# A recurrence with two MLPs behind it: the weights' working word in PSUM, scores masked on half the partitions, decay products stored with time outermost

## The chip, the cores and the metric

The kernel runs on one core of one Trainium2 chip. The core has five engines that run side by side, each through its own list of instructions in order: PE (TensorE, the matmuls), DVE (VectorE), ACT (ScalarE), POOL (GpSimd) and SP (SyncE, which mostly issues DMAs). The metric is the device time of one execution in microseconds (us), as a median of runs.

## The reference

The input `r, k, v, w, a, b` has 4 batches, 8 heads, 768 time steps and 40 channels. A 40 by 40 state per batch and head is carried over time:

```python
y[:, :, t] = einsum('bhd,bhde->bhe', rt, state)
Sa = einsum('bhde,bhe->bhd', state, at)
state = state * wt[:, :, None, :] - einsum('bhd,bhe->bhde', Sa, bt) + einsum('bhd,bhe->bhde', vt, kt)
```

Its output, 3072 tokens by 320, goes through two MLPs. The first is `g(x @ w_in) @ w_out` with 2048 hidden columns and `g(h) = h` for h >= 1, 0 for h <= -1 and (h+1)^2/4 between. The second is `(silu(x @ w_gate) * (x @ w_val)) @ w_out` with 1536. The MLP weights are 64-bit floats in DRAM; everything else is 32 bits.

## The kernel before

Time is cut into 12 chunks (`c`) of 64 steps, and each chunk into 4 super-units (`n`, one for each batch, with 8 heads), 48 in all. A planner (`Plan`) holds all work as tasks with an engine, an estimated cost, what they read and write, and which buffers they use. It simulates the engines from estimates and due times, and so settles the order of instructions on every engine; the kernel is then written out in that order. The due times come from the constants in line 1262. Buffers are handed out from pools; a pool can grow (`K.grow`) once given tasks are over.

The kinds of work:

- `decay_tasks` (lines 661 to 760), for three groups of 4 chunks: running products of the decays `w` and of their reciprocals, on 128 partitions (4 chunks x 32 batch-heads), 32 steps at a time, 40 channels a step. The tiles lie in `wg` and `wv`, the memory of the second MLP's weights, which are therefore loaded later. `last` (lines 713 to 721) copies the products at the chunk ends aside, `store` (723 to 728) writes the products to two DRAM tensors, `was` and `wks`, one pair for each group.
- `p_tasks` (785 to 880), for each n: loads r, k, a, b and, for each pair of n, 64 steps x 16 batch-heads x 40 of `was` and of `wks` (`ldw`, line 805); multiplies, splits into two 16-bit halves, turns, and forms the scores of one n with 8 matmuls (line 850) in a `pg` tile of PSUM, 128 partitions x 512. Line 853 multiplies them by the causal `mask` (which also holds a factor of 2^-6), line 857 copies the lower half to `gf`, from which line 861 stores them to DRAM (`lsd`).
- `inv_tasks` (882 to 942), for each chunk: reads `lsd` back and inverts triangular blocks with 62 small dependent steps on DVE (lines 912 and 917). Only entries right of the diagonal are read. The result goes to DRAM (`tsd`).
- `m_tasks` (970 to 1162), for each n, after the inverse of its chunk: a chain PE, ACT, DVE, PE ... through one `px` tile of PSUM (matmuls of lines 1035, 1045, 1051; ACT 1059, 1070; DVE in `xlo`, `slo`), then the output y and the next state. It reads `was` once for each pair of n (line 996). The first four n use the two `ph` tiles in place of `px`.
- The MLPs: `in1` and `in2` (matmuls of line 1167), the pointwise part on ACT, DVE and POOL (1187 to 1217), `outp` (1231).
- `wpiece` (578 to 641), 58 of them: one piece of weights is loaded as raw 64-bit words (`wr`), turned into 32-bit floats by three DVE bit operations (lines 609, 613, 617) in a 32-bit buffer `wu` in SBUF, then split into 16-bit halves by ACT (636, 629) and POOL or DVE. 28 pieces are 128 partitions x 320, 30 are 512 columns on 128 or 64 partitions. 30 pieces of the second MLP (`late`) wait until all decays are done.

PSUM has eight tiles of 128 x 512 here: two each of `px`, `pg`, `ph` and `po`. DVE and POOL tasks that the planner takes to hold the port that both share are marked `lk`.

Of the kernel before, what the change touches and what calls it, by code (L numbers as in the profile page):

```python
# [8 lines left out]
F32 = mybir.dt.float32  # L9
# [313 lines left out]
def tile_recurrence__then__gated_mlps(  # L323
# [59 lines left out]
    def pst(name, n):  # L383
        ts = [pp.tile([128, 512], F32, name=f"{name}{i}") for i in range(n)]
        K.pool(name, ts)
        return ts
# [60 lines left out]
        K.spare(nm, [mx[:, 5120 + 1024 * i:6144 + 1024 * i].rearrange(  # L447
            "p (h x) -> p h x", h=H)], early)
    K.spare("gf", [mx[:, 7168:8192].bitcast(F32).rearrange("p (h t) -> p h t", h=H)], early)
    pst("px", 2)  # L450
    pst("pg", 2)
    ph = pst("ph", 2)
    po = [pp.tile([128, 512], F32, name=f"po{i}") for i in range(2)]
# [124 lines left out]
    def wpiece(names, key, src, n, m, dst_hi, dst_lo, scale, p, fit, r=()):  # L578

        key = ("w",) + key  # L580
        K.pools["wr"]["fit"][key] = [x for f in fit for x in {
            "low": (0,), "high": (1,), "free": (2,), "late": (3, 4)}[f]]
        K.pools["wu"]["fit"][key] = [x for f in fit for x in {
            "low": (0, 4), "high": (1, 5), "free": (2,), "late": (3,)}[f] if m <= 320 or x < 4]
        raw, ux = [("wr", key)], [("wu", key)]
        shape = list(dst_hi.shape)

        def st():
            return G("wr", key)[0:n, 0:2 * m].bitcast(I32)

        def x(i):
            return st().rearrange("p (b x) -> p b x", x=2)[:, :, i]

        def u():
            return G("wu", key)[0:n, 0:m]

        def u3():
            return u() if len(shape) == 2 else u().rearrange("p (a f) -> p a f", a=shape[1])

        def load(e):  # L600
            o = st()
            if len(shape) == 3:
                o = o.rearrange("p (a f) -> p a f", a=shape[1])
            e.dma_start(out=o, in_=src)

        def bits(q):
            t = u().bitcast(I32)
            if q == 0:
                v_.tensor_scalar(
                    out=t, in0=x(1), scalar1=3, scalar2=0x3FFFFFFF,  # L610
                    op0=ALU.logical_shift_left, op1=ALU.bitwise_and)
            elif q == 1:
                v_.scalar_tensor_tensor(
                    out=t, in0=x(1), scalar=-(1 << 30), in1=t, op0=ALU.bitwise_and,
                    op1=ALU.bitwise_or)
            else:
                v_.scalar_tensor_tensor(
                    out=t, in0=x(0), scalar=29, in1=t, op0=ALU.logical_shift_right,
                    op1=ALU.bitwise_or)

        pool = n == 128 and WSP
        e_, eng, cost = side(pool, m)
        if pool:
            k, scale, scale0 = 4, 1.0, scale
        else:
            k = 3

        def hi():
            s_.activation(out=dst_hi, in_=u3(), func=AF.Copy, scale=scale)

        DMA(load, r=r, w=[(key, 0)], use=raw, p=p, dma=0.00365 * m * n / 128)
        for q in range(3):
            T("DVE", 0.06 + m * (1.04e-3 if q else 0.52e-3), lambda q=q: bits(q), r=[(key, q)], lk=True,
              w=[(key, q + 1)], use=raw + ux, p=p)
        if pool:
            T("ACT", c_s(m), lambda: s_.activation(
                out=u(), in_=u(), func=AF.Copy, scale=scale0), r=[(key, 3)], w=[(key, 4)], use=ux, p=p)
        T("ACT", c_s(m), hi, r=[(key, k)], w=[(key, 5)], use=ux, p=p)
        T(eng, cost, lk=True, emit=lambda: split(dst_lo, u3(), scale, dst_hi, e_), r=[(key, 5)],
          w=[key] + names, use=ux, p=p)  # L640
        return key
# [18 lines left out]

    def decay_tasks(g, p, dp):
        dec[g] = tuple(
            dr.tile([4, BH, C, D], F32, name=f"{nm}{g}") for nm in ("was", "wks"))
        wc = w.rearrange("b h (g c t) e -> g c (b h) t e", g=NG, c=4)[g]
        EC = 16
        e_, eng, cost = side(g, 2 * D)
        for u in range(HC // EC):
# [44 lines left out]

            def last(half=half):
                a = half(0)
                v_.tensor_copy(out=p64[:, g], in_=a[:, 2 * EC + 1])
                for i in range(4):
                    n = 4 * g + i
                    if n:
                        gg, ii = divmod(n - 1, 4)
                        v_.tensor_copy(  # L720
                            out=q0s[32 * ii:32 * ii + 32, gg], in_=a[32 * i:32 * i + 32, 0])

            def store(e, i, l0, l1, half=half, lo=lo, hi=hi):
                dst, h, o, t0 = (
                    (1, 0, 1, lo), (0, 0, EC + 1, hi), (0, 1, 0, lo), (1, 1, EC + 2, hi))[i]
                e.dma_start(
                    out=dec[g][dst].rearrange("q b t e -> (q b) t e")[l0:l1, t0:t0 + EC],
                    in_=half(h)[l0:l1, o:o + EC])

            db = [("db", key)]  # L730
# [6 lines left out]
            if EC * u + EC < HC:  # L737
                T("DVE", 0.15, keep, r=[(key, EC)], w=[("cry", g, u)], use=db, p=pu)
            else:
                T("DVE", 0.5, last, r=[(key, EC)], w=[("dl", g)], use=db, p=pu)  # L740
            T("DVE", 0.33, rec, lk=True, r=[(key, EC)], w=[(key, "r", 0)], use=db, p=pu)
            for k in range(EC - 1):
                T(eng, cost, lambda k=k, back=back: back(k), lk=True, r=[(key, "r", k)],
# [41 lines left out]
    def p_tasks(n, p):  # L785
# [19 lines left out]
        def ldw(i, src, done):  # L805
            DMA(lambda e: e.dma_start(
                out=G("ldp", pp)[0:C, i].rearrange("p j h e -> p (j h) e"),
                in_=src[c % 4, 8 * j:8 * j + 16].rearrange("h t e -> t h e")),
                r=[("dec", c)], w=[done], use=L, p=p - 4, dma=1.06)

        hs = slice(8 * j, 8 * j + 8)
# [35 lines left out]
        def mm():  # L847
# [3 lines left out]

        T("PE", 0.24, mm, r=[(key, "kbT"), ("art", n)], w=[(key, "g")], use=PG + KT + A_, p=p)
        T("DVE", c_v(512, True), lambda: v_.tensor_tensor(
            out=hc(G("pg", key)), in0=hc(G("pg", key)),
            in1=mask.unsqueeze(1).to_broadcast([128, H, C]), op=ALU.mult),
          r=[(key, "g")], w=[(key, "gm")], use=PG, p=p)
        T("ACT", c_s(512), lambda: s_.copy(out=G("gf", key)[C:128], in_=hc(G("pg", key))[C:128]),  # L857
          r=[(key, "gm")], w=[(key, "gf")], use=PG + GF, p=p)

        def st(e, hf):  # L860
            e.dma_start(
# [108 lines left out]
    def m_tasks(n, p):  # L970
# [23 lines left out]
        if j % 2 == 0:  # L994
            ps = slice(8 * j, 8 * j + 16)
            DMA(lambda e: e.dma_start(
                out=G("wa", mp).rearrange("p j h d -> p (j h) d"),
                in_=was[c % 4, ps].rearrange("h t e -> t h e")),
                r=[("dec", c)], w=[(mp, "wa")], use=WA, p=p + 4, dma=1.06)
            if not last:  # L1000
                DMA(lambda e: e.dma_start(
                    out=G("ff", mp)[q].rearrange("p j h d -> p (j h) d"),
# [256 lines left out]
                    out=out[r0:r0 + C, :], in_=o()[64 * q:64 * q + 64]),  # L1259
                    r=[(ok, tt, 1)], w=[("out", c)], use=[("u", uk)], p=p, dma=0.31)  # L1260

    PER, LEAD, PLEAD, DLEAD, WLEAD, ILEAD, WSTEP, LPRI, LSTEP, BP, BI, BM, DP, BD, P1, M1 = 69.67, 10.07, 94.28, 203.97, -27.79, 128.76, 0.3, 0.99, 2.22, -0.71, 2.76, 0.02, 10.0, 113.83, 0.0, 5.0
    SUP = PER / B

    def m0(n):
# [15 lines left out]
    for i in range(NP1):  # L1281
# [4 lines left out]
        for x in ps:  # L1286
            n = len(first)
            first.append(wpiece(
                *x, p=-WLEAD + WSTEP * n, fit=("low", "high", "free") if n < NW1 else ("low", "high")))
    late, low, high = [], list(first), list(first)  # L1290
    free = [("dec", c) for c in range(NCH)] + [("f", c) for c in range(NCH - 1)] + first[:NW1]
    for i, k in W2:
        if k < 2:
# [83 lines left out]
```

## Time and profile before

| | us |
|---|---|
| median of 3 runs | 1157.7 (1156.53 to 1158.95) |
| the profiled execution, its own time | 1156.32 |
| span of the profiled execution, first to last instruction | 1154.6 |

Busy share of the span: PE 79%, ACT 75%, DVE 67%, POOL 51%. The page cuts the span into 40 slices of 28.9 us and gives the busy share of each engine in tenths (9 is 90% or more), then the clock granted to TensorE in tenths of full speed, then the share of the DMA engines that is busy. A name as `L617` is line 617 of the kernel; `xs<-px,xs` says that a tile `xs` is written from `px` and `xs`. PE's records are modelled and a few can be missing, so its busy time is a guide. The waits name the operation that came last before the engine went on.

### The profile page before, as it was taken

The page shows a single profiled execution, that of the slowest core. Times are in us where ns is not written, and L with a number is a line of the kernel's source. Part 1 is how long each engine was busy: PE and PEld are TensorE (multiplying, and loading weights), DVE is VectorE, ACT ScalarE, POOL GpSimd, SP SyncE. Part 2 cuts the span into 40 slices and gives each one's busy share as a digit, 9 for nine tenths or more (in the row PEclk, how much of TensorE's full clock was granted, in tenths as well). Part 3 has the DMA queues.
Part 4 walks back from the last instruction along what each step waited for, and adds up shares of the span by engine and source line. Part 5 has one row for each costly group of instructions (what it writes and reads, how often), then busy time and mean ns, then how long its engine had stood idle before and what let it go on. Part 6 is the DMA issues. An engine that isn't in the chain of part 4 may idle for free.

```text
span 1154.6 us, 29904 instructions
## 1 busy us (share of the span) xinstructions
PE 916.4 (79%) x11328; PEld 748.1 (65%) x11328; DVE 776.4 (67%) x1830; ACT 864.8 (75%) x1628; POOL 587.2 (51%) x756
## 2 busy tenths in 40 slices
PE   0222548426687989999999999999999999999998
PEld 0212436324575778777777777787777877788886
DVE  7888888898889485683775756947758558342211
ACT  1675987867995888987978979889798896763422
POOL 5787875435566546544554545655535432332321
PEclk9999999557799999999999999999999999999999
DMA  9967889869886888688677768875777643311000
GB/s 228 212 175 144 196 148 204 153 143 202 172 163 130 132 130 138 121 137 123 115 121 139 128 104 137 131 140 121 125 129 128 118 89 58 65 34 32 5 15 24
DMA packets 560949, 144.64 MB, mean 125 GB/s; under 512 B 537140, under 2 KB 544820, under 8 KB 560804
## 3 DMA queue, kind: packets, MB, share of 16 engines
q1 hardware_dynamic: 519984, 134.11, 63.1%
q10 hardware_dynamic: 40820, 8.62, 4.8%
q8 instruction: 88, 1.44, 0.5%
q14 instruction: 57, 0.47, 0.1%
HBM read 74.87 MB, written 18.14 MB: 81 GB/s over the span
## 4 chain that ended last, share of the span: by engine, by line
PE 31%; ACT 16%; DVE 12%; issue 5%; DMA 5%; POOL 2%; SPq 1%; ACTq 1%; POOLq 0%; DVEq 0%
PE ph L1167 17%; PE po L1231 11%; DVE pg L917 2%; DVE ub L912 2%; ACT mx L1199 2%; ACT mx L1187 2%; ACT xs L1059 1%; PE pg L1124 1%; ACT vss L1070 1%; ACT mx L1200 1%; DVE xs L539 1%; DVE mx L1217 1%; ACT gf L857 1%; ACT ss L1137 1%; POOL mx L537 1%
## 5 line engine op out<-in xcount | busy, mean ns | idle before, releaser
L537 POOL TENSOR_TENSOR mx<-mx 128x512 f16<-128x512 f32 x168 | 196.3, 1170 | 245.7 <-ACT mx L1187 224.7
L1231 PE MATMUL po<-wo,mx 128*128 128x320 f16 x2016 | 311.8, 301 | 2.3 <-POOL mx L537 1.6
L1231 PEld LDWEIGHTS <-mx 128*128 128x128 f16 x2016 | 189.7, 98 | 70.7 <-POOL mx L537 4.3
L1167 PE MATMUL ph<-mx,w 128*128 128x256 f16 x1536 | 196.0, 281 | 14.8 <-DMA mx<-x 9.3
L1167 PEld LDWEIGHTS <-w 128*128 128x128 f16 x1536 | 149.7, 100 | 40.8 <-issue 14.0
L1167 PE MATMUL ph<-x2t,wv 128*128 128x256 f16 x1152 | 142.4, 274 | 3.4 <-DVE mx L1203 2.6
L1167 PE MATMUL ph<-x2t,wg 128*128 128x256 f16 x1152 | 141.8, 275 | 2.1 <-ACT mx L1213 2.1
L1187 ACT CAST mx<-mx 128x512 f16<-128x512 f32 x168 | 102.8, 615 | 46.0 <-DVE mx L1217 31.6
L1203 DVE SCALAR_TENSOR_TENSOR mx<-ph,mx 128x512 f32<-128x512 f32 x96 | 66.0, 689 | 86.6 <-ACT mx L1200 85.8
L1167 PEld LDWEIGHTS <-wv 128*128 128x128 f16 x1152 | 110.8, 98 | 18.6 <-issue 4.5
L1167 PEld LDWEIGHTS <-wg 128*128 128x128 f16 x1152 | 110.5, 98 | 18.4 <-issue 2.5
L917 DVE TENSOR_TENSOR pg<-pg,ub 128x126 f32<-128x126 f32 (+22 forms) x372 | 96.3, 259 | 9.9
L912 DVE SCALAR_TENSOR_TENSOR ub<-ub,pg 128x126 f32<-128x126 f32 (+22 forms) x372 | 92.4, 248 | 11.3 <-DMA ub<-lsd 1.1
L1217 DVE SCALAR_TENSOR_TENSOR mx<-ph,mx 128x512 f32<-128x512 f32 x72 | 49.5, 687 | 69.4 <-PE ph L1167 64.8
L543 POOL TENSOR_TENSOR ldp<-ldp 128x320 f32<-128x320 f32 (+1 forms) x90 | 78.9, 887 | 29.4 <-ACT ldp L819 17.6
L1059 ACT ACTIVATE xs<-px 32x320 f16<-32x320 f32 x176 | 75.0, 426 | 15.7 <-PE px L1051 6.8
L1070 ACT ACTIVATE vss<-px 32x640 f16<-32x640 f32 x88 | 61.1, 695 | 12.2 <-PE px L1045 10.3
L539 DVE SCALAR_TENSOR_TENSOR xs<-px,xs 32x320 f16<-32x320 f32 x88 | 42.5, 483 | 41.1 <-ACT xs L1059 38.3
L1199 ACT ACTIVATE mx<-ph 128x512 f32<-128x512 f32 x96 | 57.1, 595 | 15.4 <-PE ph L1167 13.9
L539 DVE SCALAR_TENSOR_TENSOR vss<-px,vss 32x320 f16<-32x320 f32 x88 | 43.4, 493 | 31.6 <-ACT vss L1070 25.7
L1200 ACT ACTIVATE mx<-mx 128x512 f32<-128x512 f32 x96 | 60.5, 630 | 3.0
L1213 ACT ACTIVATE mx<-ph 128x512 f32<-128x512 f32 x72 | 42.7, 594 | 24.8 <-PE ph L1167 23.2
(234 smaller groups left out, 1715.9 us busy)
## 6 DMA issues: line engine op xcount, KB each, us to landing
ldv<-in_v_dram SPq DMA_DIRECT2D x86, 80.0 KB
ub<-lsd SPq DMA_DIRECT2D x23, 256.0 KB
wo<-in_moe_w_out_dram SPq DMA_DIRECT2D x16, 320.0 KB
ldp<-in_b_dram SPq DMA_DIRECT2D x23, 160.0 KB
ldp<-wks SPq DMA_DIRECT2D x23, 160.0 KB
out_dram<-mx SPq DMA_DIRECT2D x45, 80.0 KB
wo<-in_moe_w_in_dram SPq DMA_DIRECT2D x7, 512.0 KB
ldp<-in_r_dram SPq DMA_DIRECT2D x22, 160.0 KB
```

What stands on the lines that cost most here:

```text
L537: e.tensor_tensor(out=out, in0=x, in1=hi, op=ALU.subtract)
L539: e.scalar_tensor_tensor(out=out, in0=x, scalar=scale, in1=hi, op0=ALU.mult, op1=ALU.subtract)
L543: e.tensor_tensor(out=out, in0=x, in1=y, op=ALU.mult)
L912: v_.scalar_tensor_tensor(out=t, in0=L()[:, j, j + 1:].unsqueeze(1).to_broadcast([128, nm, ni]), scalar=-(2.0**-10), in1=m[:, 0:nm, j:j + ...
L917: v_.tensor_tensor(out=m[:, 0:nm, j + 1:], in0=m[:, 0:nm, j + 1:], in1=t, op=ALU.add)
L1059: s_.activation(out=xs[32 * i:32 * i + 32], in_=px[32 * hf:32 * hf + 32], func=AF.Copy, scale=-(2.0**-10))
L1070: s_.activation(out=hi2(G("vss", key)[z]), in_=two(hd(G("px", key))[z]), func=AF.Copy, scale=2.0**-8)
L1167: t_.matmul(out=ps, lhsT=wts[:, wi, fs], rhs=xT[:, xi, :], start=(i == 0), stop=(i == len(plan) - 1))
L1187: T("ACT", c_s(512), lambda: s_.copy(out=G("g", key)[:, 0], in_=u2(key)), r=[(key, "u")], w=[(key, "gh")], use=U + GG, p=p)
L1199: s_.activation(out=u2(key), in_=ps2(key), func=AF.Relu, scale=2.0**-8, bias=1.0)
L1200: s_.activation(out=u2(key), in_=u2(key), func=AF.Square, scale=2.0**3)
L1231: t_.matmul(out=ps, lhsT=g[:, x, f, 128 * tt:128 * tt + 128], rhs=wo[:, 2 * i + f, y, :], start=(i == 0 and f == 0 and m == 0), stop=(i == ...
```

## The change

1. One of the two `px` tiles becomes a pool of its own, `pw`, and goes back to `px` once all late weight pieces are done. The first two bit operations of each piece write their word there, and the third reads it from there and writes `wu`. They are no longer marked `lk`, the first one's estimated cost is doubled, and `wu` is taken only at the third.
2. `was` is stored as time x batch-head x channel instead of batch-head x time x channel; `wks` keeps its order. The two loads of `was` then read rows of 16 x 40 numbers, 2560 bytes, instead of 40 numbers, 160 bytes; the stores of `was` write 160 bytes at a time instead of 16 x 160.
3. The copies in `last` go from DVE to ACT.
4. The mask is multiplied onto partitions 0 to 63 alone. ACT copies the lower half straight from the unmasked scores, with the factor 2^-6, and no longer waits for the mask.
5. The constants of the due times: decays 14.66 us earlier (group 0 another 43.73), their two halves 6.14 us apart instead of 10, the late weights due 15.32 us earlier, the first weights 0.46 us apart instead of 0.3, `p_tasks` of chunk 0 due 9.29 us later and of chunk 1 14 us earlier, `m_tasks` of chunk 0 due 9.93 us later. The whole order is planned anew from these.

```diff
-    pst("px", 2)
+    px = pst("px", 2)
+    K.pools["px"]["free"] = px[0:1]
+    K.any("pw", px[1:2], (0,))
...
         def bits(q):
-            t = u().bitcast(I32)
+            t = G("pw", key)[0:n, 0:m].bitcast(I32)
...
             else:
                 v_.scalar_tensor_tensor(
-                    out=t, in0=x(0), scalar=29, in1=t, op0=ALU.logical_shift_right,
+                    out=u().bitcast(I32), in0=x(0), scalar=29, in1=t, op0=ALU.logical_shift_right,
...
-            T("DVE", 0.06 + m * (1.04e-3 if q else 0.52e-3), lambda q=q: bits(q), r=[(key, q)], lk=True,
-              w=[(key, q + 1)], use=raw + ux, p=p)
+            T("DVE", 0.06 + m * 1.04e-3, lambda q=q: bits(q), r=[(key, q)],
+              w=[(key, q + 1)], use=raw + [("pw", key)] + (ux if q == 2 else []), p=p)
...
         dec[g] = tuple(
-            dr.tile([4, BH, C, D], F32, name=f"{nm}{g}") for nm in ("was", "wks"))
+            dr.tile(x + [D], F32, name=f"{nm}{g}")
+            for nm, x in (("was", [C, 4 * BH]), ("wks", [4 * BH, C])))
...
-                v_.tensor_copy(out=p64[:, g], in_=a[:, 2 * EC + 1])
+                s_.copy(out=p64[:, g], in_=a[:, 2 * EC + 1])
...
-                        v_.tensor_copy(
+                        s_.copy(
...
-                    out=dec[g][dst].rearrange("q b t e -> (q b) t e")[l0:l1, t0:t0 + EC],
+                    out=(x if dst else x.rearrange("t b e -> b t e"))[l0:l1, t0:t0 + EC],
...
-            out=hc(G("pg", key)), in0=hc(G("pg", key)),
-            in1=mask.unsqueeze(1).to_broadcast([128, H, C]), op=ALU.mult),
+            out=hc(G("pg", key))[0:C], in0=hc(G("pg", key))[0:C],
+            in1=mask[0:C].unsqueeze(1).to_broadcast([C, H, C]), op=ALU.mult),
...
-        T("ACT", c_s(512), lambda: s_.copy(out=G("gf", key)[C:128], in_=hc(G("pg", key))[C:128]),
-          r=[(key, "gm")], w=[(key, "gf")], use=PG + GF, p=p)
+        T("ACT", c_s(512), lambda: s_.activation(
+            out=G("gf", key)[C:128], in_=hc(G("pg", key))[C:128], func=AF.Copy, scale=2.0**-6),
+          r=[(key, "g")], w=[(key, "gf")], use=PG + GF, p=p)
...
-                in_=was[c % 4, ps].rearrange("h t e -> t h e")),
-                r=[("dec", c)], w=[(mp, "wa")], use=WA, p=p + 4, dma=1.06)
+                in_=was[:, BH * (c % 4) + 8 * j:BH * (c % 4) + 8 * j + 16]),
+                r=[("dec", c)], w=[(mp, "wa")], use=WA, p=p + 4, dma=0.6)
...
-    PER, LEAD, PLEAD, DLEAD, WLEAD, ILEAD, WSTEP, LPRI, LSTEP, BP, BI, BM, DP, BD, P1, M1 = 69.67, 10.07, 94.28, 203.97, -27.79, 128.76, 0.3, 0.99, 2.22, -0.71, 2.76, 0.02, 10.0, 113.83, 0.0, 5.0
+    PER, LEAD, PLEAD, DLEAD, WLEAD, ILEAD, WSTEP, LPRI, LSTEP, BP, BI, BM, DP, BD, P1, M1 = 69.67, 10.07, 94.28, 218.63, -27.79, 128.76, 0.46, -14.33, 2.22, -10.0, 2.76, -9.91, 6.14, 157.56, 14.0, 5.0
...
+    K.grow("px", px[1:2], late)
```

## Rows read from the trace of the kernel before

**Rows 1.** The page's 40 slices: busy tenths of PE and DVE, DMA share.

```profile
PE   0222548426687989999999999999999999999998
DVE  7888888898889485683775756947758558342211
DMA  9967889869886888688677768875777643311000
```

**Rows 2.** Stretches: length, busy PE, weight loads, DVE, ACT, POOL; clock, DMA, GB/s.

```profile
0.00:376.00 376.00, 180.34 (x2268) 143.96 (x2269) 325.02 (x754) 270.03 (x496) 237.55 (x353) 0.88 0.87 174
207.00:269.00 62.00, 17.09 (x371) 15.12 (x370) 57.85 (x141) 43.95 (x88) 20.52 (x24) 0.52 0.82 161
269.00:322.00 53.00, 40.66 (x488) 30.89 (x488) 46.08 (x72) 47.30 (x89) 32.42 (x30) 0.82 0.91 175
376.00:1011.50 635.50, 597.05 (x7709) 489.47 (x7709) 419.27 (x1026) 538.66 (x1028) 311.88 (x365) 0.99 0.71 120
```

**Rows 3.** PE in order of time: first `in1` of chunk 1, first `in2`.

```profile
269.01 8.20 PE L1167 MATMUL ph<-mx,w 128*128 128x256 f16 x48 [4.60 <-DMA mx<-x]
322.00 1.37 PE L1167 MATMUL ph<-x2t,wg 128*128 128x256 f16 x8
```

**Rows 4.** DVE time of lines 609, 613, 617 (in this order), 0 to 376 us.

```profile
0.00:376.00 376.00, 33.40 (x58) 0.88 0.87 174
...
0.00:376.00 376.00, 43.85 (x58) 0.88 0.87 174
...
0.00:376.00 376.00, 45.02 (x58) 0.88 0.87 174
```

**Rows 5.** The chain of waits in order of time, one link: start, length.

```profile
309.12 1.20 DVE wo L617
```

**Rows 6.** DVE in order of time, weight operations without a stall.

```profile
161.24 0.32 DVE L609 TENSOR_SCALAR wo<-wo 128x320 int32<-128x320 int32 x1
...
163.33 0.48 DVE L617 SCALAR_TENSOR_TENSOR wo<-wo 128x320 int32<-128x320 int32 x1
...
166.36 0.42 DVE L609 TENSOR_SCALAR wo<-wo 128x512 int32<-128x512 int32 x1
```

**Rows 7.** Operations with a PSUM operand, to 376 us: ns min/median/max, first and last start.

```profile
L853 DVE TENSOR_TENSOR pg<-pg,mask x18: 679/698/700, 53.6 to 366.3; 128x512 f32<-128x512 f32 x18
...
L873 DVE TENSOR_TENSOR lkt<-pg,lkt x16: 683/684/685, 56.8 to 368.2; 64x512 f16<-64x512 f32 x16
...
L539 DVE SCALAR_TENSOR_TENSOR xs<-px,xs x17: 482/483/485, 165.6 to 335.0; 32x320 f16<-32x320 f32 x17
```

**Rows 8.** A POOL operation in the same stretch, the same columns.

```profile
L543 POOL TENSOR_TENSOR wg<-wg x62: 343/353/800, 34.7 to 143.5; 128x80 f32<-128x80 f32 x62
```

**Rows 9.** The copies of `last` (two lines of DVE), and a small ACT operation.

```profile
L720 DVE COPY wg<-wv x11: 172/179/3108, 27.8 to 145.4; 32x40 f32<-32x40 f32 x11
...
L954 ACT ACTIVATE x<-pf x48: 235/238/245, 135.2 to 1049.3; 64x64 f16<-64x64 f32 x48
```

**Rows 10.** One `px` tile's use, chunk 1: PE and DVE in order of time.

```profile
203.10 0.43 PE L1045 MATMUL px<-xs,tt 96*32 96x40 f16 x8 [0.53 <-DVE xs L539]
...
210.38 0.46 PE L1035 MATMUL px<-vh,lkt 128*128 128x40 f16 x8
...
216.25 0.43 PE L1045 MATMUL px<-xs,tt 96*32 96x40 f16 x8
...
205.00 0.49 DVE L539 SCALAR_TENSOR_TENSOR vss<-px,vss 32x320 f16<-32x320 f32 x1 [0.22 <-ACT vss L1070]
```

**Rows 11.** DMA: the page's main queue; issue times on SP's queue; a landing on the chain.

```profile
q1 hardware_dynamic: 519984, 134.11, 63.1%
...
L726 SPq DMA_DIRECT2D was<-wv x8: 350/430/636, 21.9 to 190.4; - x8
...
L806 SPq DMA_DIRECT2D ldp<-was x21: 587/672/2687, 37.5 to 883.7; - x21
...
987.65 3.21 DMA tsd<-ub
```

More of the change, by code (lines that the diff above doesn't have):

```diff
@@ L584, in wpiece @@
             "low": (0, 4), "high": (1, 5), "free": (2,), "late": (3,)}[f] if m <= 320 or x < 4]
+        K.pools["pw"]["fit"][key] = (0,)
         raw, ux = [("wr", key)], [("wu", key)]
@@ L725, in store @@
                     (1, 0, 1, lo), (0, 0, EC + 1, hi), (0, 1, 0, lo), (1, 1, EC + 2, hi))[i]
+                x = dec[g][dst]
                 e.dma_start(
-                    out=dec[g][dst].rearrange("q b t e -> (q b) t e")[l0:l1, t0:t0 + EC],
+                    out=(x if dst else x.rearrange("t b e -> b t e"))[l0:l1, t0:t0 + EC],
                     in_=half(h)[l0:l1, o:o + EC])
@@ L739, in decay_tasks @@
             else:
-                T("DVE", 0.5, last, r=[(key, EC)], w=[("dl", g)], use=db, p=pu)
+                T("ACT", 0.6, last, r=[(key, EC)], w=[("dl", g)], use=db, p=pu)
             T("DVE", 0.33, rec, lk=True, r=[(key, EC)], w=[(key, "r", 0)], use=db, p=pu)
@@ L807, in ldw @@
                 out=G("ldp", pp)[0:C, i].rearrange("p j h e -> p (j h) e"),
-                in_=src[c % 4, 8 * j:8 * j + 16].rearrange("h t e -> t h e")),
+                in_=src[:, BH * (c % 4) + 8 * j:BH * (c % 4) + 8 * j + 16] if i == 3 else
+                src[BH * (c % 4) + 8 * j:BH * (c % 4) + 8 * j + 16].rearrange("h t e -> t h e")),
                 r=[("dec", c)], w=[done], use=L, p=p - 4, dma=1.06)
```

## The prediction

> **What bounds the kernel now.** I read the page's slices first [rows 1]. From about slice 13 on PE is at 8 or 9 tenths; before it PE is mostly idle while DVE stands at 7 to 9 and the DMA engines likewise. The cut by stretches says the same in microseconds [rows 2]: in 376 us PE is busy for 180, DVE for 325 (86%), ACT for 270, POOL for 238. From 376 to 1011 PE is busy 597 of 635.5 us, and the last five slices are nearly PE alone [rows 1]. So the kernel is two programs: a head of 376 us in which PE waits for weights, decays and the recurrence, and a tail in which PE's own work sets the pace. What the head gives back moves the end nearly one for one, because the tail behind it is the same matmuls and the recurrence is over some 100 us before the end.
>
> Within the head the worst place is 207 to 269 us: PE does 17 us of work at a granted clock of 0.52 (mostly the 1.2 GHz level) after a stretch of sparse matmuls, while DVE is busy 57.85 of 62 us, 93% [rows 2]. PE then waits for the tokens of chunk 1 (269 us) and for the second MLP's weights: `in2` of chunk 0 starts at 322 [rows 3]. All three bit operations of all 58 weight pieces fall into the head; they take 33.40 + 43.85 + 45.02 = 122.3 us, 38% of DVE's time there [rows 4]. The chain of waits, as far as it can be followed back (to 303 us), runs through them too, by a link of 1.20 us for one [rows 5].
>
> **The bit operations.** Undisturbed, an operation on 320 columns takes 0.32 (line 609) or 0.48 us, on 512 columns 0.42 us for line 609 [rows 6]; by the sums the three lines take 0.58, 0.76 and 0.78 on average [rows 4]. Operations on DVE with one operand in PSUM do not vary at all: 512 columns 683 to 685 ns or 679 to 700, 320 columns 482 to 485, over the same 376 us [rows 7]. POOL's decay steps, with everything in SBUF, show the counterpart: median 353 ns and up to 800 [rows 8]. I read this as DVE and POOL holding each other up where DVE's operands all lie in SBUF, and not where one lies in PSUM. After the change each of the three has an operand or its result in PSUM. So 28 pieces x 3 x 0.483 = 40.6 and 30 x 3 x 0.684 to 0.698 = 61.6 to 62.8 make 102 to 103 us; rounded up to 104, that saves 18 of 122. Line 609 itself gets dearer: 28 x (0.48 - 0.32) + 30 x (0.68 - 0.42) = 12 us, already in the 104. Bounds: 20 gained; or 12 lost, if the stalls stay and only line 609's price comes. I take 18, since the rows of the same shape with a PSUM operand are flat.
>
> **The copies of `last`.** DVE loses line 720's 11 copies at 0.18, one of them stalled to 3.1, some 5 us, and three more of about 0.2 from line 715: 5.5 us [rows 9]. ACT gains 14 at about 0.24 [rows 9], 3.4 us, beside other work, as ACT is 72% busy in the head [rows 2]. The new wait: ACT now stands at the end of each decay chain, which POOL runs for groups 1 and 2 at 353 ns a step [rows 8]; behind it on ACT are the copies out of PSUM. Bounds 0 to 3 us for each of the two groups; I take 0, because DVE had no idle time worth naming ahead of these copies.
>
> **Mask and `gf`.** Halving the partitions saves nothing: 64 partitions x 512 take 684 ns, 128 take 698 [rows 7]. `gf` starts one mask earlier, 0.7 us once per chunk on the way to the inverse; of the first four chunks, which PE awaits, 0 to 2.8 us in all. I take 1.
>
> **`was` in DRAM.** The main queue moves 519984 packets and 134.11 MB in 63.1% of 16 engines' span [rows 11], that is 22.4 ns a packet or 13.9 ns for 160 bytes. A load of `was` is 1024 rows of 160 bytes: 0.9 (by bytes) to 1.4 us (by packets) of all 16 engines; after, 64 rows of 2560: 0.1 to 0.9. A store of 128 partitions goes the other way: 128 rows today, 0.2 to 1.8 us, 2048 rows after, 1.8 to 2.9. There are 48 loads but only about 18 in the head, and the equal of 12 such stores, all in the head. So the head gains 0 to 23 us of DMA time and loses 0 to 32; I take nothing there, as the middles nearly cancel. On SP's queue a load's issue falls from 0.67 us towards the 0.43 of a 128-row store, 4 us in the head; 16 stores grow from 0.43 to somewhere between that and twice a load's 0.67, 0 to 15 us over the first 190. For chunk 0 the cover is the gap between its stores, the last of them from `wv` from 21.9 us on, and the first load at 37.5 [rows 11]. If that cover were gone, a store's landing would count whole: 64 KB in runs of 64 bytes landed in 3.21 us [rows 11], so 2048 runs in at most 6.4.
>
> The Trainium skill speaks against this part: "DMA: Bandwidth & Descriptors", section Specifications, says that below 512 bytes the DMA engine reads and rewrites what it writes. The row nearest to it, 1024 writes of 64 bytes in 3.21 us, shows no such price so far; if the rule holds at full weight it is the fourth rival below.
>
> **One `px` tile.** This is the cost. In chunk 1 the first two n hold both tiles and wait for the inverse; the second's first matmul of line 1045 runs at 203.10, while the first n is done at 205.49 [rows 10]. With one tile the second n can only start its chain then, and a chain takes 5.9 us from its first matmul to that point (210.38 to 216.25) [rows 10]. That is 205.5 + 3 to 5.9 = 208.5 to 211.4 instead of 203.1: 5 to 8 us late, and the two n behind it likewise. The next chunk in the head has the same pattern. The delay doesn't add up from chunk to chunk, since each waits for its own inverse. Bounds 0 to 8 us on the start of `in1`; I take 4, as at 93% DVE fills such gaps with work that it owes anyway. No wait is added between pieces: reuse of the PSUM word is in order on DVE.
>
> **The order.** The constants ask for decays, and the second MLP's weights behind them, some 15 us earlier. By how much DVE can comply is bounded by its load. It is 0 in the sum, and a rival.
>
> **Sum.** DVE loses 18 + 5.5 = 23.5 of its 325 us in the head. I pass on 86% of it, its busy share: 20 us, and 1 for `gf`. Less 4 for `px`: 17. The tail I take as it was; shorter loads and an earlier `gf` could touch its 38 us of PE gaps, but nothing there waits for them for long. The profiled execution took 1156.32 us (1154.6 span and 1.7 around it), so 1139; the median lies 1.4 higher: 1140.5.
>
> **Rivals.** (a) *More than that.* If the weights of the second MLP come early enough, `in2` of chunk 0 fills the hole from 215 to 322 us, where PE idles 45 + 12 us. One chunk of it is 96 + 96 matmuls at about 0.27 and some 72 at 0.3, about 73 us, so the hole could be filled; but DVE still owes most of its time. I give 17 + 25 = 42 us, the 25 being less than half of those 57: 1116. For: the low clock there, which would go too. Against: DVE at 93%.
> (b) *DVE was busy but not late.* The chain goes over ACT, PE and landings as well, ACT is busy 72%, and freed DVE time becomes idle time: 2 to 6 us, 1153.
> (c) *The one `px` tile decides, and it is slower.* In a head with the recurrence as the late thing, 8 us are lost for each of two chunks that then do follow each other, and DVE's 23.5 us go unused except for some 8: 16 - 8 = +8, 1165. It decides as soon as `in1` of chunk 1 starts later than 269 us.
> (d) *The small stores are dear.* By bytes from 64 KB in 3.21 us [rows 11], 320 KB would need 16 us. The DMA engines stand at 6 to 9 tenths or more in the first seven slices [rows 1]; if each of the 12 stores took twice 2.9 us of all engines there instead of at most 1.8, 48 us of DMA time would be added, a third of it late, and the gain is eaten: 1157.
> (e) *It doesn't do what it says.* The stalls come from another side than the operands, line 609 gets dearer by 12 us, and 12 - 5.5 = 6.5 us more DVE work, and 4 to 8 for `px`, make 1165.
>
> **How the numbers follow.** Forecast, 1128 to 1151: 0.50. (a) 1105 to 1128: 0.15. (b) 0.14, of which 0.04 is too small to see. (d) 0.04. (c) 0.12 and (e) 0.05. A measurement of this kernel can tell about 0.2%, 2.3 us, from no change. Faster by more: 0.50 + 0.15 + 0.10 = 0.75; same 0.04 + 0.04 = 0.08; slower 0.17. The range leaves out the best part of (a) and the worst of (c) and (e): 1112 to 1163.
>
> **What would show it.** Lines 609, 613 and 617 flat near 0.49 and 0.69 us and 104 us in sum; POOL's maxima smaller; `in1` of chunk 1 before 269 and `in2` of chunk 0 before 322; the last weight piece some 17 us earlier than 376. PE waiting on line 1035 for `slo` of the n before would speak for (c); ACT or landings in place of DVE in the head's waits for (b); late first loads of `was` for (d). The prediction is wrong if DVE's time falls and the second MLP starts no earlier, or if the tail's gaps change: I have taken the tail as fixed, and the new order touches it too.

## The result, and the profile after

The kernel after takes 1166.53 us (median of 4 runs, 1165.09 to 1167.19), the kernel before, run beside it, 1157.86 (1156.53 to 1158.95). The ratio is 1.0068, 95% interval 1.0047 to 1.0089: slower by 0.7%, 8 to 9 us, where 1140.5 was predicted with a range up to 1163.

The part of the forecast on DVE itself came true. The three bit operations by shape, of the kernel after (count | busy us, mean ns of one | idle before); 320 and 512 columns now have one price each, in every line:

```profile
L612 DVE TENSOR_SCALAR px<-wo 128x320 int32<-128x320 int32 x17 | 8.3, 486 | 3.9 <-DMA wo<-in_moe_w_out_dram 3.8
L616 DVE SCALAR_TENSOR_TENSOR px<-wo,px 128x320 int32<-128x320 int32 x17 | 8.4, 491 | 0.3
L612 DVE TENSOR_SCALAR px<-wo 128x512 int32<-128x512 int32 x14 | 9.6, 686 | 3.5 <-DMA wo<-in_moe_w_in_dram 3.4
L620 DVE SCALAR_TENSOR_TENSOR wo<-wo,px 128x512 int32<-128x512 int32 x13 | 8.9, 684 | 0.5
```

The same three lines (612, 616, 620 in this order, once 609, 613, 617) summed from 0 to 376 us, which answers to [rows 4]:

```profile
0.00:376.00 376.00, 34.17 (x58) 0.76 0.90 174
0.00:376.00 376.00, 34.37 (x58) 0.76 0.90 174
0.00:376.00 376.00, 34.00 (x58) 0.76 0.90 174
```

That is 102.5 us, where 104 was predicted and 122.3 stood before. The stretches of the kernel after (length, busy PE, weight loads, DVE, ACT, POOL; clock, DMA share, GB/s), to be read against [rows 2]:

```profile
0.00:376.00 376.00, 172.95 (x2280) 140.30 (x2281) 297.58 (x737) 273.25 (x509) 224.44 (x362) 0.76 0.90 174
207.00:269.00 62.00, 20.07 (x365) 16.58 (x364) 55.17 (x135) 43.13 (x84) 21.64 (x25) 0.54 0.79 144
269.00:322.00 53.00, 37.38 (x466) 28.98 (x464) 45.02 (x77) 47.38 (x90) 28.88 (x33) 0.89 0.84 171
```

DVE is busy for 297.6 us instead of 325.0, 27 less (the prediction: 23.5). POOL, for which the prediction had no term, gains as well: 224.4 instead of 237.6. The last weight operation starts at 352.4 instead of 374.4 us. Yet PE got through 2280 matmuls by 376 us, against 2268: the head is hardly further. The landmarks of [rows 3] in the kernel after, `in1` of chunks 1 and 6 and `in2` of chunk 0 (start, length, idle before it):

```profile
267.19 1.23 PE L1174 MATMUL ph<-mx,w 128*128 128x256 f16 x5 [5.03 <-DMA mx<-x]
...
317.59 1.04 PE L1174 MATMUL ph<-x2t,wg 128*128 128x256 f16 x8
...
693.76 2.53 PE L1174 MATMUL ph<-mx,w 128*128 128x256 f16 x11 [2.82 <-DMA mx<-x]
```

`in1` of chunk 1 comes 1.8 us earlier, `in2` of chunk 0 4.4 us. So 27 us of DVE and 13 of POOL gave 2 to 4. And then the tail loses: `in1` of chunk 6 starts at 693.8 us where it started at 689.1, chunk 7 at 772.4 instead of 762.4, and from there on all is 9 to 11 us late. The tail by stretches, first before, then after (columns as above):

```profile
376.00:690.00 314.00, 291.35 (x3766) 237.53 (x3765) 207.30 (x510) 268.11 (x510) 162.29 (x194) 0.99 0.76 126
690.00:850.00 160.00, 152.36 (x1988) 125.79 (x1987) 107.86 (x261) 139.86 (x268) 84.63 (x99) 1.00 0.77 133
```

```profile
376.00:690.00 314.00, 288.30 (x3707) 234.77 (x3707) 208.05 (x509) 266.57 (x505) 158.61 (x185) 0.99 0.77 124
690.00:850.00 160.00, 147.11 (x1908) 119.93 (x1907) 104.83 (x257) 135.04 (x258) 78.77 (x92) 0.99 0.71 127
```

Behind 376 us the kernel after does 59 and 80 fewer matmuls in these two stretches. What PE lacked is on the page, in the group of the first MLP's matmuls (busy, mean | idle before it and its releaser), before and after:

```profile
L1167 PE MATMUL ph<-mx,w 128*128 128x256 f16 x1536 | 196.0, 281 | 14.8 <-DMA mx<-x 9.3
```

```profile
L1174 PE MATMUL ph<-mx,w 128*128 128x256 f16 x1536 | 191.2, 277 | 29.6 <-DMA mx<-x 18.2
```

`mx<-x` are the turned tokens, the output of the recurrence. PE waits twice as long for them. And the inverses, on which the recurrence waits, are late too; the end of the inverse of each chunk (the last of its 62 steps in the trace, us) and the time of the same execution, with five of the kernels below:

| chunk | 3 | 4 | 5 | 6 | 7 | 11 | time |
|---|---|---|---|---|---|---|---|
| before | 371.7 | 442.0 | 514.9 | 594.4 | 671.9 | 983.5 | 1156.3 |
| after | 370.7 | 448.7 | 532.8 | 610.9 | 682.7 | 995.0 | 1167.1 |
| prio_before | 372.1 | 443.6 | 517.7 | 593.0 | 670.7 | 984.1 | 1157.2 |
| head_before | 372.2 | 440.3 | 517.4 | 593.2 | 670.6 | 988.9 | 1161.2 |
| early_inv | 368.7 | 438.9 | 517.8 | 596.7 | 671.4 | 990.6 | 1161.8 |
| short_third_op | 368.3 | 439.1 | 512.0 | 589.2 | 666.5 | 977.9 | 1151.0 |
| long_second_op | 394.6 | 466.2 | 539.0 | 616.2 | 693.7 | 1005.7 | 1178.4 |

Up to chunk 3 the two kernels are level. The 7 to 18 us at chunks 4 to 6 show behind the head, where no weight piece runs any more, and prio_before, with the same edits, doesn't have them: this is the new order, not the edits. In all seven the execution ends 171 to 173 us behind its last inverse (chunk 11), and so it does in the nine other kernels of this document. Whatever a kernel loses or gains here it has lost or gained by its last inverse; what PE does behind it takes the same time in each, within 2 us. What holds the inverses up is not in these numbers, as their steps stand in DVE's queue between other work.

### The profile page after: what moved, and what is told of

It is laid out like the page before. It is cut to its first block, busy times and chain, and to the rows that moved or that the text cites. A ratio compares the mean times of both kernels' runs of the same rounds, so it can differ in the third digit from the quotient of the medians.

```text
span 1165.4 us, 29896 instructions
## 1 busy us (share of the span) xinstructions
PE 912.2 (78%) x11328; PEld 746.0 (64%) x11328; DVE 751.7 (65%) x1816; ACT 870.4 (75%) x1642; POOL 570.2 (49%) x756
## 5 line engine op out<-in xcount | busy, mean ns | idle before, releaser
L1174 PE MATMUL ph<-mx,w 128*128 128x256 f16 x1536 | 191.2, 277 | 29.6 <-DMA mx<-x 18.2
L1194 ACT CAST mx<-mx 128x512 f16<-128x512 f32 x168 | 102.5, 615 | 51.4 <-DVE mx L1224 28.6
L545 POOL TENSOR_TENSOR ldp<-ldp 64x320 f32<-64x320 f32 (+1 forms) x90 | 76.3, 861 | 15.1 <-ACT ldp L825 9.5
L539 POOL TENSOR_TENSOR x<-pf,x 64x320 f16<-64x320 f32 x48 | 37.9, 789 | 68.2 <-ACT x L960 53.1
L539 POOL TENSOR_TENSOR vss<-ldv,vh 128x320 f16<-128x320 f32 x48 | 38.5, 802 | 59.4 <-ACT vh L1022 36.5
## 6 DMA issues: line engine op xcount, KB each, us to landing
wo<-in_moe_w_in_dram SPq DMA_DIRECT2D x7, 512.0 KB
```

Of the source, the lines that this page charges most:

```text
L539: e.tensor_tensor(out=out, in0=x, in1=hi, op=ALU.subtract)
L545: e.tensor_tensor(out=out, in0=x, in1=y, op=ALU.mult)
L1174: t_.matmul(out=ps, lhsT=wts[:, wi, fs], rhs=xT[:, xi, :], start=(i == 0), stop=(i == len(plan) - 1))
L1194: T("ACT", c_s(512), lambda: s_.copy(out=G("g", key)[:, 0], in_=u2(key)), r=[(key, "u")], w=[(key, "gh")], use=U + GG, p=p)
```

## Experiments: the edits and the order apart

Ratios are to the kernel before, run beside each, with 95% intervals. First the edits without the word in PSUM, in exactly the old order:

```diff
 # the kernel before; was, half mask, gf and last as in the change, the planner's inputs as they were
-                v_.tensor_copy(out=p64[:, g], in_=a[:, 2 * EC + 1])
+                s_.copy(out=p64[:, g], in_=a[:, 2 * EC + 1])
...
-            dr.tile([4, BH, C, D], F32, name=f"{nm}{g}") for nm in ("was", "wks"))
+            dr.tile(x + [D], F32, name=f"{nm}{g}")
```

> The kernel before with parts 2, 3 and 4 of the change in the instructions alone: was with time outermost, the copies of last on ACT, half mask and gf straight from the scores. The planner is told nothing of it (old costs, old dependences), so the order of all tasks is that of the kernel before. Word in SBUF, two px tiles. Theory A: these parts are small by themselves, 1152 to 1159 us. Theory B, if it is the stores, ACT or gf: 1163 or more.

1154.78 us, 0.9989 (0.9972 to 1.0005). The stores of 160 bytes, the longer rows of the loads, `last` on ACT and the half mask together move nothing that can be measured.

Then all edits, but with the priorities that won for the kernel before in place of those that follow from the new constants:

```diff
 # the kernel after, Plan.run
-        prio, best = [t["p"] for t in self.tasks], None
-        for _ in range(self.rounds):
+        prio, best = [x / 1000 for x in PRIO], None   # the old kernel's winning priorities
+        for _ in range(1):
```

> All edits of the change stay (word in PSUM, one px tile in the head, was with time outermost, last on ACT, half mask). Only the priorities by which the planner orders the tasks are those with which it won in the kernel before, task by task, written into the kernel as a list. Theory A (the new order of the recurrence's tasks is what lengthens the tail; the edits themselves are worth something): faster than before, 1140 to 1152 us, with the inverse of chunk 5 ending before 515 us (before: 514.9, after: 532.8). Theory B (the edits cost it: one px tile, or dearer stores, or more on ACT): as slow as the changed kernel, 1162 to 1170.

1156.97 us, 1.0014 (0.9997 to 1.0032), between the two expectations. The order costs the kernel after some 0.5%: the intervals 0.9997 to 1.0032 and 1.0047 to 1.0089 don't meet. But in a good order the change brings nothing either, though DVE is busy for 300.6 us here instead of 325.0. Two questions, then: where do DVE's microseconds go, and what is wrong with the order.

A new plan from the old constants says that the new constants are not to blame as such:

```diff
 # the kernel after with the old line of constants
-    PER, LEAD, PLEAD, DLEAD, ... = 69.67, 10.07, 94.28, 218.63, ...
+    PER, LEAD, PLEAD, DLEAD, ... = 69.67, 10.07, 94.28, 203.97, ...
```

> The changed kernel with the constants of the kernel before (part 5 undone), planned anew. Its order is then neither before's nor after's. Theory A: the time goes with the order found, and no order is found that is as good as before's: 1162 to 1185, with the inverses of chunks 4 to 7 later than before's. If the constants alone were to blame for the loss (the prediction's edits being worth 17 us): 1140 to 1150.

1176.51 us, 1.0185 (1.0159 to 1.021). Three orders of the same work span 20 us.

## Experiments: what DVE's time is worth

Putting the word back into SBUF, in the order of the kernel after and in that of prio_before:

```diff
-    K.any("pw", px[1:2], (0,))
+    K.any("pw", [sb.tile([128, 512], F32, name="pw")], (0,))
```

> The changed kernel with one edit: the word of the first two bit operations lies in a tile of its own in SBUF and not in the px tile; px keeps one tile until the weights are done, and the order of all tasks is that of the changed kernel. DVE's bit operations should vary again and take 115 to 130 us in sum instead of 102.5. If the head's DVE time reached the end one for one, as the prediction put it (86%), the end is 10 to 22 us later: 1177 to 1189. If the head is paced by the tokens of the recurrence and the weights have slack, 0 to 6 us: 1166 to 1173.

1181.92 us, 1.0245 (1.0207 to 1.0284). The bit operations take 122.1 us again instead of 102.5.

> prio_before (the change's edits, planned from the old kernel's priorities, one px tile), with the working word in an SBUF tile of its own instead of the px tile; nothing else differs from prio_before. Theory A (the word's place is worth some 15 us in any order, the single px tile costs about as much): 1157 + 15 = 1168 to 1176. Theory B (in this order DVE's time is not late): 1155 to 1160, as prio_before.

1174.65 us, 1.0168 (1.015 to 1.0186); 123.7 us instead of 102.6. So 20 and 21 us more on DVE go with 15 to 21 (by medians or by ratios) and 18 at the end: the 86% of the prediction, so far. But they are not DVE's alone. POOL gets dearer with them, by 18.8 us in word_sbuf (the pages of the kernel after and of word_sbuf, busy us) and by 20.2 in prio_before_sbuf:

```profile
PE 912.2 (78%) x11328; PEld 746.0 (64%) x11328; DVE 751.7 (65%) x1816; ACT 870.4 (75%) x1642; POOL 570.2 (49%) x756
PE 909.5 (77%) x11328; PEld 744.8 (63%) x11328; DVE 774.3 (66%) x1816; ACT 870.8 (74%) x1642; POOL 589.0 (50%) x756
```

These two runs price the word's place, not DVE's time. Next, DVE time taken away in the old order, both `px` tiles kept:

```diff
 # the kernel before, third bit operation
-                    out=t, in0=x(0), scalar=29, in1=t, op0=ALU.logical_shift_right,
+                    out=t[:, 0:16], in0=x(0)[:, 0:16], scalar=29, in1=t[:, 0:16], op0=ALU.logical_shift_right,
```

> The kernel before, its order and both px tiles untouched; only the third bit operation of every weight piece works on 16 columns instead of 320 or 512, so the low three bits of most weights stay zero. That takes some 40 of the 45 us of line 617 off DVE in the head, more than the change does. Theory A (DVE time of the head reaches the end, and what eats it with the old priorities is the single px tile): 86% of 40 us, 1157 - 34 = about 1123, in any case 1115 to 1138. Theory B (with the old order DVE is busy but not late; loads, tokens and the inverse pace the head): 1150 to 1157, in1 of chunk 2 still near 370.

1149.97 us, 0.9952 (0.9933 to 0.997). The bit operations fell from 122.3 to 93.7 us, so 28.6 us less on DVE (and 7 less on POOL), and the end gained 5.6: 20%. Where the rest went is seen at one place. Before the scores at 264 us PE and its weight loads stand still for 8.3 us; the kernel before, in order of time:

```profile
258.73 1.24 SPq L768 DMA_TRANSPOSE kbT<-kbs  x1
...
263.80 0.45 PEld L850 LDWEIGHTS <-kbT 120*128 120x128 f16 x8 [8.39 <-DMA kbT<-kbs]
263.81 0.61 PE L850 MATMUL pg<-art,kbT 120*128 120x64 f16 x8 [8.27 <-DVE wo L617]
```

and short_third_op:

```profile
255.03 1.24 SPq L768 DMA_TRANSPOSE kbT<-kbs  x1
...
260.25 0.45 PEld L850 LDWEIGHTS <-kbT 120*128 120x128 f16 x8 [8.54 <-DMA kbT<-kbs]
260.26 0.61 PE L850 MATMUL pg<-art,kbT 120*128 120x64 f16 x8 [8.42 <-DMA kbT<-kbs]
```

In the kernel before line 617 is named as the releaser, the one long wait of PE on a bit operation between 207 and 322 us. With that operation cut to 16 columns the wait is as long as before, and now the transpose by DMA is named, which the weight load beside it had named all along: some 5 us from the start of its issue on SP's queue to the matmul. The whole stretch has moved by 3.5 us, no more.

So the word put back costs about as much as the DVE time that it adds, and time taken off gives 20%. Is that the direction, or do the new orders hang on DVE where the old one doesn't? Two runs with opposite answers:

```diff
 # the kernel before: long_second_op, behind the second bit operation
+                h = m // 2
+                v_.scalar_tensor_tensor(
+                    out=t[:, 0:h], in0=x(1)[:, 0:h], scalar=-(1 << 30), in1=t[:, 0:h], op0=ALU.bitwise_and,
+                    op1=ALU.bitwise_or)
 # the kernel after: after_short_second
-                    out=t, in0=x(1), scalar1=3, scalar2=0x3FFFFFFF,
+                    out=t, in0=x(1), scalar1=0, scalar2=-(1 << 25) - 1,
...
-                    out=t, in0=x(1), scalar=-(1 << 30), in1=t, op0=ALU.bitwise_and,
+                    out=t[:, 0:16], in0=x(1)[:, 0:16], scalar=-(1 << 30), in1=t[:, 0:16], op0=ALU.bitwise_and,
```

> The kernel before, its order and both px tiles untouched; the second bit operation of every weight piece is done once more on half of its columns, which changes no bit of the result and adds 20 to 27 us to DVE in the head. Theory H (any of these orders is balanced so that several things come due together: DVE time taken away exposes the next one, DVE time added is late at once): 80% of it reaches the end, as with word_sbuf and prio_before_sbuf, 1173 to 1179. Theory I (the old order doesn't hang on DVE, the new ones do): 20% of it, 1160 to 1164.

1178.36 us, 1.0202 (1.0167 to 1.0237). The bit operations take 154.3 us, 32.0 more, and the end is 23 us later: 72%. POOL's busy time is 2 us above the kernel before, so this is the run that prices DVE's time by itself.

> The kernel after, its order untouched; the second bit operation works on 16 columns only (the first keeps other bits of the word, so that the values stay small; the weights are wrong), which takes some 28 of its 34.4 us off DVE. Theory H: 20% of it reaches the end, 1166.5 - 6, 1158 to 1163. Theory I (the new orders hang on DVE): 80%, 1166.5 - 22, 1142 to 1148.

1162.99 us, 1.0051 (1.0027 to 1.0076), against 1.0068 for the kernel after. The second operation takes 10.0 us instead of 34.4; of 24.4 us taken off, 2 to 4 reach the end, and the two intervals overlap, so that even these are not clear of noise. It is the direction: in the old order by 72% against 20%, and in the new one time taken off pays as little. The releasers of PE's waits from 207 to 322 us in the kernel before show why (total us, times, longest):

```profile
PE px L1045 <- DVE xs L539: 10.5, 6, 3.4
PE pg L850 <- DVE wo L617: 8.3, 1, 8.3
PE px L1035 <- ACT vh L1015: 6.1, 2, 5.1
PE px L1051 <- DVE vss L539: 5.3, 3, 2.7
PE px L1035 <- POOL vss L537: 5.0, 5, 1.6
PE pg L1103 <- DVE lkt L873: 4.7, 1, 4.7
PE ph L1167 <- DMA mx<-x: 4.6, 1, 4.6
```

Behind the one wait on a bit operation stand links of the recurrence over DVE, ACT, POOL and DMA, a few us each. With fewer bit operations one gets shorter and another longer: in short_third_op `xs` falls from 10.5 to 8.8 us and `mx<-x` grows from 4.6 to 6.9, and all of PE's waits in this stretch make 58.7 us, against 57.4. Each queue is worked off in a fixed order, so whatever comes later than planned holds up what is queued behind it, while what comes earlier waits for the next of these links. That last step is a reading of the waits; the runs show the two prices.

## Experiments: one `px` tile, and the DMA engines

```diff
 # the kernel before, planned from its own winning priorities
-    pst("px", 2)
+    px = pst("px", 2)
+    K.pools["px"]["free"] = px[0:1]
...
+    K.grow("px", px[1:2], late)
```

> The kernel before with nothing changed but that one of the two px tiles is withheld until the late weights are done (no one uses it in the meantime); bit operations, stores and copies as before, planned from the old kernel's priorities. Theory A (one tile costs what the prediction put, 4 to 8 us): 1160 to 1166. Theory B (one tile costs as much as the word in PSUM is worth, about 18 us; that is why prio_before_sbuf is at 1175): 1171 to 1178. Theory C (the tile costs nothing; prio_before_sbuf is late because its order was made for shorter bit operations): 1155 to 1159.

1162.68 us, 1.0049 (1.0033 to 1.0065): 5.7 us lost. The place is the one that the prediction read in [rows 10]. In one_px the second n of chunk 1 starts its chain when the first gives the tile back (PE in order of time; lines 1272 and 1282 are 1035 and 1045 of the kernel before):

```profile
205.18 0.47 PE L1272 MATMUL px<-vh,x2t 128*128 128x40 f16 x8
...
208.60 0.35 PE L1282 MATMUL px<-xs,tt 96*32 96x40 f16 x8 [1.22 <-DVE xs L776]
...
218.28 0.42 PE L1272 MATMUL px<-vh,lkt 128*128 128x40 f16 x8 [2.90 <-DVE vss L776]
...
231.67 0.42 PE L1272 MATMUL px<-vh,lkt 128*128 128x40 f16 x8 [3.84 <-DVE vss L776]
```

208.60 us instead of 203.10, and the next two n wait 2.9 and 3.8 us for the one before. The prediction had 208.5 to 211.4.

So prio_before looks like the sum of +5.7 for the tile and about -6 for the word. The -6 is what short_third_op gained with more DVE time taken off; from one_px to prio_before, with the same priorities, the word and the smaller edits together give 4 (by ratios) to 6 (by medians). prio_before_sbuf has these priorities too, one tile, and bit operations of 123.7 us where one_px has 124.6, but it is 12 us later than one_px. What differs besides the small edits, worth nothing in same_order, is what the planner was told: of the small edits, and of the bit operations (their cost, their buffers and the mark `lk`). So the 18 us of prio_before_sbuf hold for an order that was planned for a word in PSUM; why that order suffers more isn't shown.

The DMA engines are as busy in the head as DVE [rows 2]. Here a weight piece whose raw buffer already held a piece of that size loads only half of its columns, once alone and once with short_third_op:

```diff
 # the kernel before, load in wpiece
+            i = src
...
+            if any(n <= y and m <= z for y, z in seen):
+                f = o.shape[-1] // 4 * 2
+                o, i = (o[:, :, 0:f], i[:, :, 0:f]) if len(shape) == 3 else (o[:, 0:f], i[:, 0:f])
...
-            e.dma_start(out=o, in_=src)
+            e.dma_start(out=o, in_=i)
```

> The kernel before, its order untouched; a weight piece whose raw buffer has already held a piece of that size loads only half of its columns (the other half keeps older words). All other work, DVE's too, stays. It takes about 10 of some 65 MB off the DMA engines in the head, where they stand at 87% to 90%. Theory D (the DMA engines pace the head): 1157 - 20 to 40, 1117 to 1138. Theory B (neither DVE nor DMA alone paces it; the chain of the recurrence through the engines' fixed orders does): 1149 to 1157, as short_third_op.

1152.85 us, 0.9964 (0.9944 to 0.9985). The head from 0 to 376 us moves 151 GB/s with the DMA engines at 77%, against 174 and 87% [rows 2]:

```profile
0.00:376.00 376.00, 184.26 (x2279) 146.48 (x2280) 326.92 (x754) 271.15 (x498) 238.55 (x354) 0.87 0.77 151
```

About a tenth of the head's DMA time is worth 4 us.

> light_loads and short_third_op in one kernel, the order of before. If DVE and DMA take turns as what is late (the one hides the other), the two together give clearly more than the sum of both alone: 1140 or less. If each gives its own few us and something else paces the head, the sum: 1143 to 1151.

1147.52 us, 0.9909 (0.9882 to 0.9936): 10 us, the sum of the two. They don't hide each other; neither of the two resources that look full paces the head. The Trainium skill ("Perfetto Trace Analysis", section "Identifying the Most-Contended Engine") says to work first on the engine of highest occupancy. In this head that paid little: of the compute engines DVE is the busiest there, at 86%, and 28.6 us off it gave 5.6.

## Experiments: the order

Both runs are the kernel after with a written list of priorities, 6067 numbers; in words, the lists are:

- head_before: the old kernel's priority if the task is planned to start before 380 us, else that of the kernel after;
- early_inv: that of the kernel after, less 10 us for a task of `p_tasks` or `inv_tasks` of chunks 4 to 7.

> The change's edits; tasks that the plan of prio_before starts before 380 us take the old kernel's priorities, all others those of the kernel after. If the 9.5 us between the kernel after and prio_before arise from the order of the head (the inverses and p_tasks of chunks 3 to 6 are already put off there): 1154 to 1160. If they arise from the order of the tail (690 to 850 us, where after falls behind): 1163 to 1170.

1158.83 us, 1.0021 (1.0001 to 1.0042). Most of the loss is gone with the order of what is planned before 380 us, which holds the `p_tasks` of chunk 4, and the inverses of chunks 4 to 7 end as in prio_before (table above). The two lists differ by a median of 87 us, so at the seam the head's tasks also go first; the run can't tell these apart.

> The kernel after; only the priorities of the p_tasks and inverses of chunks 4 to 7 are 10 us earlier. In the plan their inverses then end at 398, 471, 541 and 607 us instead of 407, 479, 549 and 615, while the planner's own forecast of the end hardly moves (1068.1 for 1069.4). Theory E (the kernel after is late because its order puts the inverses of chunks 4 to 7 off, and the recurrence never makes that up): most of the 9.5 us come back, 1156 to 1161. Theory F (it is not these alone, the end follows the planner's forecast for the whole order): 1164 to 1167.

1160.15 us, 1.0046 (1.003 to 1.0062). By medians two thirds of the 9.6 us between the kernel after and prio_before come back, by ratios two fifths, and the interval still meets that of the kernel after. The inverses of chunks 4 to 7 end 10 to 15 us earlier than in the kernel after (table above), as in prio_before; from chunk 8 on, where no priority was moved, that is half lost again: 753.7 us, with 746.0 in prio_before and 759.3 in the kernel after. That the late inverses are a cause fits the medians and the table, in which the time follows the last inverse; the ratios leave it open, and that they are the only cause isn't shown.

Last, an order searched for by varying the priorities of prio_before at random, with the planner's own forecast of the end as the measure:

> The change's edits in an order found by varying the priorities of prio_before at random and keeping what the planner's own forecast likes: 1054.1 us where prio_before has 1062.9, the kernel after 1069.4 and old_const 1081.8. These three took 94, 97 and 95 us more on the chip than their forecast. Theory F (for the same tasks the end follows the forecast): 1054 + 95 = 1149, 1146 to 1152. Theory G (a forecast this far tuned is fitted to estimates that the chip doesn't keep; the in-order queues give the gain back): 1155 to 1165.

1157.78 us, 1.0015 (0.9993 to 1.0037). The forecast fell by 8.8 us from prio_before, the time not at all. Up to there forecast and time had gone together (1062.9, 1069.4, 1081.8 and 1157, 1166.5, 1176.5 us). An order tuned further on the planner's estimates gained nothing here. It also shows that PE's wait for the tokens is no measure of the loss: the matmuls of `in1` wait 21.5 us for `mx<-x` in searched and 12.0 in prio_before, and the time is the same. No version here beats the kernel before with its full work.

## Why the prediction was wrong, step by step

- *Bit operations* (-18 us of DVE; measured 122.3 to 102.5, -20): right, and right for its reason, the flat rows with a PSUM operand. POOL, the other side, got 17 us shorter over the whole kernel (587.2 to 570.2), which the sum left out. The Trainium skill ("SBUF — State Buffer", section "Who interferes with whom") says that a DVE instruction with two inputs in SBUF contends with a POOL instruction that reads SBUF. The traces agree that both lose time there: lines 613 and 617, with two such inputs, took 0.16 and 0.19 us per operation more than with the word in PSUM ([rows 4] against the sums after).
- *Copies of `last`, mask, `was`*: nothing in the sum but 1 us for `gf` and 5.5 us of DVE; same_order measures 0.9989 with 7.8 us less on DVE in the head. That the small stores are dear, rival (d), is out.
- *"I pass on 86% of it, its busy share"*: the step that failed first. It made 20 us of 23.5. Measured are 20% (5.6 of 28.6) in the old order and about a tenth in the new. This is 14 to 15 us of the miss of 26. Rival (b), "DVE was busy but not late", had this at 2 to 6 us, and one wait of the kind that it named, 4.6 us of PE on a landing, already stood in [rows 3]; the one link of 1.20 us in [rows 5] was thin ground for the other reading. Time added to DVE comes nearer to the 86%: 72% in long_second_op.
- *One `px` tile* (4 us, bounds 0 to 8): 5.7, the term slightly too small. Rival (c) was right that it eats what DVE gives, though by 6 against 6 and not by 16 against 8, and its sign, `in1` of chunk 1 later than 269 us, did not come (267.2).
- *"It is 0 in the sum"*, the order, and the tail *"as it was"*: the second step that failed. prio_before to after is 0.5% by ratios and 9.6 us by medians, and it lies behind 376 us, where the text had PE's own work set the pace. PE's busy share there (94%) is no proof of that: the end follows the last inverse at 171 to 173 us in every kernel here, and in the kernel after that inverse is 11.5 us late (995.0 against 983.5). With the old order the tail does pass on what the head gives, as the prediction had it: the inverse of chunk 3 comes 3.4 us earlier in short_third_op and 22.9 later in long_second_op, and the executions end 5.4 earlier and 22.1 later. The prediction had named the sign itself, "if the tail's gaps change".
- Together: -6 for the word, +6 for the tile, 0 for the rest and +6 to +10 for the order make +6 to +10; measured +8 to +9. The number 1165 of rival (c) came near for a reason that holds only in part, and that of rival (e), which is also 1165, for one that doesn't hold, as the bit operations did get shorter.
- A reading beside the sum was wrong too: the low clock of 207 to 269 us did not come "after a stretch of sparse matmuls". The slice of 173 to 202 us before it has PE at 8 tenths [rows 1], the busiest slice up to there.

## What to carry to other kernels

A busy share says what an engine has to do, not what its time is worth: ask PE's waits who ends them, look at the weight load beside the matmul when the releaser is an engine that does short work, and expect microseconds taken off a queue in a balanced order to pay less than microseconds added to it cost (here 20% and 72%). A change that lets a planner order everything anew carries a price of its own, here as large as that of any edit; measure the edits in the old order first. Here the planner's forecast told bad orders from good ones, and could not choose between good ones.

## What was not expected of the hardware

- The time that a DVE operation on SBUF loses beside POOL doesn't grow with its size, on average. The third operation of short_third_op, on 16 columns (ns min/median/max):

```profile
L617 DVE SCALAR_TENSOR_TENSOR wo<-wo x34: 157/190/1119, 22.2 to 288.7; 128x16 int32<-128x16 int32 x28, 64x16 int32<-64x16 int32 x6
```

  All 58 take 18.8 us, 0.17 us each above the shortest; at full width they took 45.0 against 34.0 with the word in PSUM, 0.19 each. Short operations paid about as much as long ones.
- TensorE's granted clock in the head is 0.88 in the profiled execution of the kernel before and 0.76 in that of the kernel after. It isn't the change that lowers it, as both kernels have executions near a mean clock of 0.91 and near 0.96 (the kernel before: 1154.36 us at 0.914, 1154.82 at 0.959). And it cost nothing that can be seen: four runs of the kernel after at a mean clock of 0.918, 0.920, 0.914 and 0.964 took 1167.1, 1165.1, 1165.9 and 1167.2 us, the highest clock the longest.
- Stores of 160 bytes in place of 2560, and the reverse for loads, leave the main queue's share about where it was, though with as many bytes it has 19200 packets fewer (same_order, against [rows 11]):

```profile
q1 hardware_dynamic: 500784, 134.11, 62.5%
```

  In the first 104 us, where many of the stores lie, the DMA engines' share rises from 0.89 to 0.94 in same_order, at the same 191 GB/s; the end doesn't notice.
